# Later low parts, other split points and other slots in a kernel of attention plus product-key experts

## The chip, the cores and the metric

The kernel runs on one core of a Trainium2 chip. Its metric is device time in microseconds (us), the median of several executions. Engines are named as in the profile: PE (TensorE), ACT (ScalarE), DVE (VectorE), POOL (GpSimd), and SP, whose queue issues most of the transfers. Each engine carries out its own instructions strictly in the order in which the program lists them, and waits where an operand or a buffer is not ready.

## What is computed

```python
x = A_x                                   # 2048 tokens x 512
xn = layernorm(x)
A = softmax(q k / 4) v  @ wo              # 32 heads of 16, one key and one value head (k, v = xn @ wk, xn @ wv)

q = einsum("nd,dhc->nhc", xn, w_q)        # 32 heads, 2 x 128
s1, s2 = q[..., :128] @ k1.T, q[..., 128:] @ k2.T      # 64 scores each
# the two best of s1 and the two best of s2 -> 4 sums -> the two best of these: expert i1 * 64 + i2 of 4096
g = softmax(the two sums)
act = gelu(einsum("nd,nhkd->nhk", xn, u[experts]))
B = einsum("nhk,nhk,nhkd->nd", g, act, v[experts])
out = x + A + B
```

## The kernel before

The whole order of instructions is written out by hand. A main loop of 280 steps `d` carries the attention: in a step, `att_steps` computes scores for two key tiles of a unit of four heads and 512 queries, ACT takes their exponentials (`scores`, L448 and L455), and PE adds the previous ones to the output (`pv`, L465). Between these, `fill()` lets one generator, the score thread, go on by about 4 cost units, and `mid()` puts the DVE work of the step in place. What the score thread lists is fixed by its own costs and not by measured times.

The score thread works through `SEQ`: 4 phases of 512 tokens times 8 chunks `c` of 4 heads. For a pair (phase, chunk), `item` computes the 8 x 64 scores of 128 tokens with 12 matmuls (L699): for each quarter k of the 512 features three products of high and low half-precision parts, `TERMS`. DVE then finds the best (MAX8, L712) and their places (FIND_INDEX8, L714) and frees the scores' buffer. `batch` follows each chunk's four items: it turns places into expert numbers with small operations, so far on POOL.

The chunks' weights come from `wp_make`, a generator advanced twice in each item of the chunk before, once after its sixth matmul and once behind it: four steps multiply `w_q` with the keys (L644), four steps (one for each k) transpose the result (L657), and ACT and DVE write its high part (L659) and low part (L660). `wp_square` sums squares of the next chunk's raw weights on ACT (L615). Scores, transposes and most other short products share three PSUM buffers, tag "x" (`xtile`); a new one waits until the oldest content has been read.

Phases 0 and 1 serve the experts by gathering: POOL fetches the rows of one expert choice for 128 tokens, DVE takes a dot product (L1192) and later adds the weighted row (L1227). One such choice is a *slot*, 512 in all; `pos` in the main loop says how many slots may have had their dot by step d, with a rate that depends on `dense_on`, the stage of the score thread.

Phases 2 and 3 serve the experts densely, in `dense`. First `spread` transposes the index and gate tables (L940), then 32 *one-hot* steps `q` build, on DVE, tables of ones (`oh`, `obs`, L973 to L976) that PE multiplies into a gate for every expert (L1012). After that come 32 *blocks* `b` of 128 experts: PE multiplies tokens with a block's u rows (`pact`, L915), ACT and DVE apply gelu and gates, and PE multiplies with the v rows (`pout`, L1058). A block needs its rows split into high and low parts (`half_split`, ACT L874 and DVE L877). In phase 2 the raw rows are fetched (`fetch`, L832 and L833) into one of two buffers; `later_split(b)` splits block b at the next `mid()` and puts `fetch(b + 2)` into the stores of the main step after the next:

```python
        def later_split(b):
            def go():
                split(b)
                store(lambda: store(lambda: fetch(b + 2)))
            on_act(go)
```

If `split(b)` finds that the fetch has not been issued, it issues all waiting stores there and then. In phase 3 the split rows are loaded from memory as phase 2 left them. `SPLITS` names the one-hot steps (NQ = 32) at which the first blocks are split; later ones are split from within the blocks. `dense_on` is 4 and 2 during the last items and the one-hot steps, 3 at their end, 1 in the blocks from b = 4 on, and 0 otherwise. In the program's stores, SP's queue issues transfers in the order in which `run(STORES)` meets them.

Of the kernel before, what the change touches and what calls it, by code (L numbers as in the profile page):

```python
# [23 lines left out]
P = 128  # L24
# [9 lines left out]
NC = 8  # L34
TPH = GT
NPH = NGRP
NSP = 2
# [23 lines left out]
def tile_kernel(ctx, tc, x, wq, wkv, wo, wqT, kT, uv, ub, vb, out):  # L61
    nc = tc.nc
# [4 lines left out]
    late = [None]  # L67
# [6 lines left out]
    raw = lambda ap: ap  # L74
# [4 lines left out]
    d_w = [dram.tile([P, KC, 2, 512], F16, name=f"dw{c}") for c in range(NC)]  # L79
# [55 lines left out]
    XT, XS, XK, XN, ACC, XP = [], {}, {}, {}, {}, [None]  # L135
    STORES, BULK, AFTER, LASTQ = [], [], [], []
    store = STORES.append
# [68 lines left out]
                BULK.append(lambda k=k, xt=xt: nc.sync.dma_start(d_xt[g - 1][k], raw(xt[:])))  # L206

    TERMS = ((0, 0), (0, 1), (1, 0))

    FIRST = ((0, 0), (1, 0), (0, 1))  # L210
    cols = const.tile([P, 40], F32, name="cols")
# [383 lines left out]
    WC = {}  # L595
# [31 lines left out]
    def wk_tile():  # L627
        return big.tile([P, 2, 512], F16, name="wk", tag="wk", bufs=NWK)

    def wp_make(c):  # L630

        wt = [big.tile([P, 2, 512], F32, name="wt", tag="da", bufs=2) for _ in range(2)]
        for h in range(4):
            for n in range(4 * c + h + 1, min(4 * c + h + 5, 4 * NC) if late[0] else 4):
                if ("raw", n // 4, n % 4) not in WC:
                    wp_load(n // 4, n % 4)
            if c == 2 and h > 1:
                wp_square()
            if c > 2 and h == 1:
                wp_factors()  # L640
            w = WC.pop(("raw", c, h))
            p = xtile("pw")
            for s in range(2):
                nc.tensor.matmul(p[s * E:(s + 1) * E, :], kTs[:, s, :], w[:, s, :], start=True, stop=True)  # L644
            nc.scalar.copy(wt[h // 2][:, h % 2, :], p)
            yield 0.9
        WC[c] = []
        if c == 2:
            yield 0.05
            wp_factors()  # L650
            yield 0.05
        for k in range(KC):
            for _ in range((0, 2, 1, 1)[k] if 1 < c < NC - 1 else 0):
                wp_square()
            p = xtile("pwt")
            for h in range(4):
                nc.tensor.transpose(p[:, h * P:(h + 1) * P], wt[h // 2][:, h % 2, k * P:(k + 1) * P], ident)  # L657
            wk = wk_tile()
            nc.scalar.activation(wk[:, 0, :], p, AF.Copy, scale=col(S_W + c))  # L659
            low = lambda p=p, wk=wk: nc.vector.scalar_tensor_tensor(wk[:, 1, :], p, col(S_W + c), wk[:, 0, :],  # L660
                                                                    op0=OP.mult, op1=OP.subtract)
            if c == 1 and late[0] is None:
                AFTER.append(low)
            else:
                low()
            WC[c].append(wk)
            (store if c > 1 else BULK.append)(lambda k=k, wk=wk: nc.sync.dma_start(d_w[c][:, k], raw(wk[:])))
            yield 0.45

    def wp_read(n, ks=range(KC)):  # L670
        for k in ks:
# [9 lines left out]
    def item(n_, ti, make=()):  # L681
        ph, c = SEQ[n_]
        nph, nc_ = SEQ[n_ + 1] if n_ + 1 < len(SEQ) else (None, None)
        t = TPH * ph + ti
        g, j = divmod(t, GT)
        b, jb = divmod(ti, BT)
        if jb == 0:
            m8 = small.tile([P, BT, 8, 8], F32, name="m8", bufs=1)
            i8 = small.tile([P, BT, 8, 8], U32, name="i8", bufs=1)
            M8[ph, c, b], I8[ph, c, b] = m8, i8  # L690
        m8, i8 = M8[ph, c, b], I8[ph, c, b]
        p = xtile("psc")

        more = nc_ is not None and not (ph >= NSP and c == NC - 1)
        read = more and n_ + 1 >= NC
        n = 0
        for k in range(KC):
            for a, bb in TERMS:
                nc.tensor.matmul(p, XT[k][:, a, j * P:(j + 1) * P], WC[n_][k][:, bb, :],  # L699
                                 start=n == 0, stop=n == 11)  # L700
                n += 1
            if read and ti == 0 and k < 2:
                wp_read(n_ + 1, range(2 * k, 2 * k + 2))
            if k < KC - 1:
                yield 3 * UNIT
            if k == 1 or k == 0 and n_ == 1:

                yield from islice(make, 1)
        if more and nph != ph:
            load_xt(nph, j)  # L710
        for s in range(8):
            nc.vector.max(m8[:, jb, s, :], p[:, s * E:(s + 1) * E])  # L712
        for s in range(8):
            nc.vector.max_index(i8[:, jb, s, :], m8[:, jb, s, :], p[:, s * E:(s + 1) * E])  # L714
        if jb == BT - 1:
            batch(ph, c, b)
        yield 3 * UNIT

    IDX, G = {}, {}
# [11 lines left out]
    def batch(ph, c, b):  # L731
# [6 lines left out]
        V = nc.vector  # L738
# [15 lines left out]
            LATER.append(go)  # L754

        fi = T("fi", F32, [P, BT, 8, 2])
        G_ = nc.gpsimd
        G_.tensor_copy(fi, i8[:, :, :, 0:2])  # L758
        fv = fi.rearrange("p t (h s) k -> p t h s k", s=2)
        i1a, i1b, i2a, i2b = fv[:, :, :, 0, 0], fv[:, :, :, 0, 1], fv[:, :, :, 1, 0], fv[:, :, :, 1, 1]  # L760
# [3 lines left out]
        if ph < NSP:  # L764
            idx = T("idx", I32, [P, BT, 4, 2], NIDX)
            i1 = fv[:, :, :, 0, :]
            G_.tensor_scalar(i1, i1, float(E), None, op0=OP.mult)
            G_.tensor_add(e1, i1a, i2b)
            G_.tensor_add(e2, i1b, i2a)
            G_.tensor_add(i1a, i1a, i2a)  # L770
            G_.tensor_sub(e1, e1, e2)
            G_.tensor_mul(e1, e1, cond)
# [51 lines left out]
    def dense(DG, after):  # L824
# [67 lines left out]
# [5 lines that stand above are left out]
# [4 lines left out]
        NQ = 512 // TB  # L901
# [9 lines left out]
        def activations(b, us, p):  # L911
            n = 0
            for k in range(KC):
                for a, c in TERMS:
                    nc.tensor.matmul(p, us[:, a, k * P:(k + 1) * P], XT[k][:, c, :],  # L915
# [53 lines left out]
        def onehot(q):  # L969
            if q < NQ:  # L970
# [6 lines left out]
                OH[q] = oa, ob  # L977

        half = lambda b: on_act(lambda: halves.__setitem__(b, half_split(b, 0)))
        SPLITS = {NQ - 18: lambda: later_split(0), NQ - 15: lambda: later_split(1),  # L980
                  NQ - 12: lambda: half(2), NQ - 10: lambda: later_split(2),
                  NQ - 8: lambda: half(3), NQ - 6: lambda: later_split(3),
                  NQ - 4: lambda: half(4), NQ - 2: lambda: later_split(4)}

        def first_gates():

# [16 lines left out]
        for q in range(NQ):  # L1003
# [5 lines left out]
            p = xtile("pg")  # L1009
            for i in range(TB):  # L1010
                n = 2 if i < TB - 1 else 1
# [24 lines left out]

            if q in SPLITS:
                SPLITS[q]()
            if q == NQ - 3:
# [7 lines left out]
        def sums(group, to):  # L1047
# [5 lines left out]
            for j in range(GT):  # L1053
                p = xtile("pout")
                n, last = 0, 3 * len(group) - 1
                for wd, vs in group:
                    for a, c in TERMS:
                        nc.tensor.matmul(p, wd[0][:, a, j * P:(j + 1) * P], vs[:, c, :], start=n == 0, stop=n == last)  # L1058
# [15 lines left out]
        for b in range(NB):  # L1074
            wd = []
            if b > 1:
                if b not in halved:

                    yield None
                if b not in halved:  # L1080
                    flush()
                p = xtile("pact")
                for k in activations(b, splits[b][0], p):
                    if k == 0:
                        store(lambda b=b: (fetch_gates(b + 1), fetch_gates(b + 2)))
                        if b % 2 == 0 and b > 2:
                            later_split(b + 2)
                        if b == 2:

                            store(load_totals)  # L1090
                    if k == KC - 1 and b == NB - 1 and after is not None:
                        wp_read(after, range(2))
                    if b == NB - 1 and after is not None:
                        load_xt(SEQ[after][0], ks=(k,))
                    if k < KC - 1:
                        yield 3 * UNIT

                if b not in fetched:
                    if formed[0] < b // 2 * 2 - 4:
                        flush()  # L1100
                    run(STORES)
                    assert b in fetched
# [44 lines left out]
            for _ in range(b - 1 if b in (2, 3) else 0):  # L1147
                if out_ready():
                    block_out()
                    yield 3.6  # L1150
            if b % 2 and b > 1:
                later_split(b + 2)
            if b > 4 and b % 4 == 1 or b == NB - 1:
                n = 4 if b < NB - 1 else 2
# [14 lines left out]
    NSL = len(slots)  # L1169
# [92 lines left out]
    def run(fns):  # L1262
        todo = fns[:]
        fns.clear()
        for fn in todo:
            fn()
# [92 lines left out]
    dense_on, quiet = [0], [0]  # L1359
# [215 lines left out]
    with tc.manual_schedule(engines=ENGINES):  # L1575
# [4 lines left out]
        half = STEPS // 2  # L1580
        pos, since = 0.0, half
        for d in range(half + 24):


            if dense_on[0] != 0:
                since = d
            if dense_on[0] == 1:
                pos += 2.5 if d < half * 3 // 4 else max(0.0, NSL - pos) / max(half - 3 - d, 1)
            else:
                pos += (2.5 if len(IDX) < NC * TPH else 2.3 if 0 <= d - since < 32 else 1.75, 0, 0.5, 1.5, 0.5)[dense_on[0]]  # L1590

            todo = max(min(int(pos + 0.001), g_next[0]) - d_next[0], 0) if d else 0

# [74 lines left out]
def build(nc, tc, args):  # L1668
    tile_kernel(tc, *args)
# [33 lines left out]
```

## Time and profile before

| | us |
|---|---|
| median of 3 runs | 1810.38 |
| lowest and highest | 1809.15 and 1815.13 |
| profiled execution, its own time | 1814.29 |
| span in that profile, first to last instruction | 1812.6 |
| PE busy | 1705.5 |
| DVE busy | 1592.4 |
| ACT busy | 1328.8 |
| POOL busy | 685.1 |

The span is cut into 40 slices; digits are tenths of busy time, and PEclk is the granted clock of PE in tenths:

```
PE   7989998999998889999999999999998899999998
DVE  7748898999998976899899899999999868989995
PEclk9999999999999999999999999999998999999999
```

The two darker places of PE in the middle and near three quarters are the one-hot stages. In the answers shown below, a row of the order of time is: start, duration, engine, line, operation, output and input, count, and in brackets the idle time ahead and who ended it. A row of waits is: who waited for whom, total us, times, longest.

### The profile page before, as it was taken

To read this page: it belongs to the slowest core of one execution; us is meant where nothing else is said; L and a number is where in the kernel's file an instruction comes from. 1 tells how busy PE (TensorE), PEld (TensorE's weight loads), DVE (VectorE), ACT (ScalarE), POOL (GpSimd) and SP (SyncE) were. 2 spreads that over 40 slices of the span, in tenths; PEclk is the share of its full clock that TensorE was granted. 3 is DMA by queue.
4 is the path that set the end of the run, shared out by engine and by line. 5 is a ranking of instruction groups with operands and counts; after the bars stand their busy time and mean duration, and the time that the engine had idled before them with its cause. 6 is when DMAs were issued, how large, how long until landed. Compare 5 with 4: busy or idle time off the path is not lost.

```text
span 1812.6 us, 35046 instructions
## 1 busy us (share of the span) xinstructions
PE 1705.5 (94%) x11070; PEld 601.1 (33%) x11070; DVE 1592.4 (88%) x6337; ACT 1328.8 (73%) x1793; POOL 685.1 (38%) x923
## 2 busy tenths in 40 slices
PE   7989998999998889999999999999998899999998
PEld 3433332333333332333333333332333333333332
DVE  7748898999998976899899899999989868989995
ACT  6467787877767886888888666655667877777774
POOL 1034353445543012344344455445541124544440
PEclk9999999999999999999999999999998999999999
DMA  7378788999764567899999976777443789999893
GB/s 260 125 254 308 264 279 282 316 321 324 270 212 139 169 230 260 284 313 341 302 334 345 330 280 237 237 245 245 149 159 131 224 263 293 324 292 332 290 311 114
DMA packets 257273, 470.98 MB, mean 260 GB/s; under 512 B 107316, under 2 KB 118596, under 8 KB 257084
## 3 DMA queue, kind: packets, MB, share of 16 engines
q0 software_dynamic: 73728, 268.47, 43.2%
q1 hardware_dynamic: 182940, 199.59, 34.4%
q8 instruction: 87, 1.43, 0.3%
q14 instruction: 102, 0.84, 0.1%
q10 hardware_dynamic: 416, 0.66, 0.1%
HBM read 407.36 MB, written 56.39 MB: 256 GB/s over the span
## 4 chain that ended last, share of the span: by engine, by line
PE 58%; DVE 20%; ACT 8%; issue 3%; DMA 3%; POOL 1%; SPq 0%; ACTq 0%; DVEq 0%; another core or an unknown queue 0%; POOLq 0%
PE pv L465 17%; PE sc L448 10%; PE psc L699 10%; PE pout L1058 8%; PE pact L915 7%; ACT pt L455 5%; DVE i L714 4%; DVE xa L1227 3%; DVE m L712 3%; DVE g L1192 3%; PE pwo L565 2%; DVE oh L973 2%; PE pw L644 1%; ACT wk L874 1%; DMA rsb<-dinv 1%
## 5 line engine op out<-in xcount | busy, mean ns | idle before, releaser
L455 ACT ACTIVATE pt<-sc 128x1024 f32<-128x1024 f32 x1024 | 990.1, 1026 | 336.6 <-PE sc L448 299.2
L1180 POOL DMA_INDIRECT g<-in_uv_dram,idx x512 | 544.6, 1064 | 896.7 <-DVE xa L1227 367.8
L465 PE MATMUL pv<-pt,vaug 128*32 128x512 f32 x4096 | 503.6, 610 | 0.0
L1227 DVE SCALAR_TENSOR_TENSOR xa<-g,w,xa 128x512 f32<-128x512 f32 x512 | 372.2, 745 | 0.0
L699 PE MATMUL psc<-wk,xt 128*128 128x512 f16 x1536 | 358.4, 381 | 12.5 <-DVE i L714 7.2
L448 PE MATMUL sc<-qa,kaug 64*128 64x512 f16 x2048 | 325.6, 385 | 40.0 <-ACT pt L455 35.3
L1192 DVE CUSTOM_DVE_ANT_0 g<-g,xa 128x512 f32<-128x512 f32 x512 | 334.3, 682 | 2.6 <-DMA g<-in_uv_dram,idx 2.6
L699 PEld LDWEIGHTS <-xt 128*128 128x128 f16 x1536 | 140.9, 98 | 210.9 <-issue 63.0
L448 PEld LDWEIGHTS <-kaug 64*128 64x128 f16 x2048 | 82.0, 94 | 381.7 <-issue 377.9
L714 DVE FIND_INDEX8 i<-m,psc 128x8 uint32<-128x64 f32 x1024 | 206.4, 222 | 0.0
L465 PEld LDWEIGHTS pv<-pt,vaug 128*32 128x32 f32 x4096 | 108.2, 110 | 259.8 <-issue 259.8
L915 PE MATMUL pact<-xt,wk 128*128 128x512 f16 x768 | 184.3, 385 | 4.2 <-DVE wk L877 3.9
L1058 PE MATMUL pout<-wk,wd 128*128 128x512 f16 x768 | 176.5, 380 | 0.0
L712 DVE MAX8 m<-psc 128x8 f32<-128x64 f32 x1024 | 146.1, 214 | 7.9 <-PE psc L699 7.2
L915 PEld LDWEIGHTS <-wk 128*128 128x128 f16 x768 | 69.6, 99 | 105.3 <-issue 29.3
L1058 PEld LDWEIGHTS <-wd 128*128 128x128 f16 x768 | 73.2, 98 | 93.3 <-issue 9.3
L973 DVE TENSOR_TENSOR oh<-io,tr 128x2048 f16<-128x2048 f16 x64 | 77.9, 1218 | 10.0 <-PE pg L1012 4.7
L714 DVE MATCH_VALUE_LOAD i<-m,psc 128x8 f32 x1024 | 72.1, 70 | 0.0
L1131 DVE SCALAR_TENSOR_TENSOR gy<-gy,pact 128x512 f32<-128x512 f32 x60 | 41.0, 683 | 30.2 <-ACT gy L1130 29.0
L1061 DVE SCALAR_TENSOR_TENSOR da<-pout,cols,da 128x512 f32<-128x512 f32 x72 | 53.3, 746 | 15.3 <-PE pout L1058 14.4
L758 POOL CAST fi<-i 128x64 f32<-128x64 uint32 x32 | 8.2, 257 | 141.7 <-DVE i L714 137.9
L1110 DVE SCALAR_TENSOR_TENSOR gy<-gy,gates 128x512 f32<-128x512 f32 x60 | 41.4, 690 | 22.1 <-ACT gy L1132 17.3
(218 smaller groups left out, 1464.6 us busy)
## 6 DMA issues: line engine op xcount, KB each, us to landing
wk<-dw SPq DMA_DIRECT2D x96, 256.0 KB
wqt<-in_wqT_dram SPq DMA_DIRECT2D x32, 512.0 KB
un<-in_uv_dram SPq DMA_DIRECT2D x16, 1024.0 KB
ds<-wk SPq DMA_DIRECT2D x64, 256.0 KB
gates<-dg SPq DMA_DIRECT2D x64, 256.0 KB
wk<-ds SPq DMA_DIRECT2D x64, 256.0 KB
dg<-gst SPq DMA_DIRECT2D x14, 928.0 KB
dw<-wk SPq DMA_DIRECT2D x32, 256.0 KB
```

Of the source, the lines that this page charges most:

```text
L448: nc.tensor.matmul(p[:, b, :], kaug[o:o + 64, kc * P:(kc + 1) * P], QA[u][o:o + 64, i, :], start=True, stop=True)
L455: nc.scalar.activation(PT[u, kc, i], p, AF.Exp, scale=SCALE)
L465: nc.tensor.matmul(PV[u][32 * j:32 * j + 32, :], vaug[:, kc, :], pt[:, b, :], start=kc == 0, stop=kc == 15)
L699: nc.tensor.matmul(p, XT[k][:, a, j * P:(j + 1) * P], WC[n_][k][:, bb, :], start=n == 0, stop=n == 11)
L712: nc.vector.max(m8[:, jb, s, :], p[:, s * E:(s + 1) * E])
L714: nc.vector.max_index(i8[:, jb, s, :], m8[:, jb, s, :], p[:, s * E:(s + 1) * E])
L915: nc.tensor.matmul(p, us[:, a, k * P:(k + 1) * P], XT[k][:, c, :], start=n == 0, stop=n == 11)
L973: nc.vector.tensor_tensor(out=oa, in0=num(P), in1=bc(0, tb, P), op=OP.is_equal)
L1058: nc.tensor.matmul(p, wd[0][:, a, j * P:(j + 1) * P], vs[:, c, :], start=n == 0, stop=n == last)
L1180: nc.gpsimd.indirect_dma_start(out=gt, out_offset=None, in_=uv, in_offset=bass.IndirectOffsetOnAxis(ap=IDX[ph, c, ti][:, s:s + 1], axis=0))
L1192: nc.vector.tensor_tensor_reduce(u, u, XN[TPH * ph + ti], scale=1.0, scalar=0.0, op0=OP.mult, op1=OP.add, accum_out=a[:, i:i + 1])
L1227: nc.vector.scalar_tensor_tensor(acc, v, w[:, i:i + 1], acc, op0=OP.mult, op1=OP.add)
```

## The change

It moves work and changes no product. Low parts and their store are listed one step of `wp_make` later, and a chunk's first item uses the products with new low parts as late as it can (`LOWS_LAST`). Each of the four transposing steps has one `wp_square` instead of none, two, one and one. In the last chunk of phases 2 and 3 the index operations are DVE's instead of POOL's. The splits of the first blocks are put at other one-hot steps: block 4's leaves them for block 2's first step, block 5's comes from block 3's end to its first step. The rates of `pos` change: 2.6 for 2.5 in the blocks, 2.3 for 20 instead of 32 steps after a dense stage, 0.25 for 0.5 in one-hot steps.

```diff
+    LOWS_LAST = ((0, 0, 0), (0, 1, 0), (1, 0, 0), (1, 1, 0), (2, 0, 0), (2, 1, 0),
+                 (0, 0, 1), (1, 0, 1), (3, 0, 0), (3, 1, 0), (2, 0, 1), (3, 0, 1))
...
         for k in range(KC):
-            for _ in range((0, 2, 1, 1)[k] if 1 < c < NC - 1 else 0):
+            run(lows)
+            if 1 < c < NC - 1:
                 wp_square()
...
-            if c == 1 and late[0] is None:
-                AFTER.append(low)
+            if c == 0:
+                low()
             else:
-                low()
+                (AFTER if late[0] is None else lows).append(low)
             WC[c].append(wk)
-            (store if c > 1 else BULK.append)(lambda k=k, wk=wk: nc.sync.dma_start(d_w[c][:, k], raw(wk[:])))
+            keep = lambda k=k, wk=wk: nc.sync.dma_start(d_w[c][:, k], raw(wk[:]))
+            if late[0] is None:
+                BULK.append(keep)
+            else:
+                lows.append(lambda keep=keep: (store if c > 1 else BULK.append)(keep))
             yield 0.45
+        run(lows)
...
-            for a, bb in TERMS:
-                nc.tensor.matmul(p, XT[k][:, a, j * P:(j + 1) * P], WC[n_][k][:, bb, :],
+            for kk, a, bb in LOWS_LAST[n:n + 3] if ti == 0 else [(k, *ab) for ab in TERMS]:
+                nc.tensor.matmul(p, XT[kk][:, a, j * P:(j + 1) * P], WC[n_][kk][:, bb, :],
...
-        G_ = nc.gpsimd
+        G_ = V if ph >= NSP and c == NC - 1 else nc.gpsimd
...
-        SPLITS = {NQ - 18: lambda: later_split(0), NQ - 15: lambda: later_split(1),
-                  NQ - 12: lambda: half(2), NQ - 10: lambda: later_split(2),
-                  NQ - 8: lambda: half(3), NQ - 6: lambda: later_split(3),
-                  NQ - 4: lambda: half(4), NQ - 2: lambda: later_split(4)}
+        SPLITS = {NQ - 16: lambda: later_split(0), NQ - 12: lambda: later_split(1),
+                  NQ - 6: lambda: half(2), NQ - 4: lambda: half(3),
+                  NQ - 2: lambda: later_split(2), NQ - 1: lambda: later_split(3)}
...
-                        if b % 2 == 0 and b > 2:
+                        if b % 2 == 0 or b == 3:
                             later_split(b + 2)
...
-            if b % 2 and b > 1:
+            if b % 2 and b > 3:
                 later_split(b + 2)
...
-                pos += 2.5 if d < half * 3 // 4 else max(0.0, NSL - pos) / max(half - 3 - d, 1)
+                pos += 2.6 if d < half * 3 // 4 else max(0.0, NSL - pos) / max(half - 3 - d, 1)
             else:
-                pos += (2.5 if len(IDX) < NC * TPH else 2.3 if 0 <= d - since < 32 else 1.75, 0, 0.5, 1.5, 0.5)[dense_on[0]]
+                pos += (2.5 if len(IDX) < NC * TPH else 2.3 if 0 <= d - since < 20 else 1.75, 0, 0.25, 1.5, 0.5)[dense_on[0]]
```

More of the change, by code (lines that the diff above doesn't have):

```diff
@@ L646, in wp_make @@
             yield 0.9
-        WC[c] = []
+        WC[c], lows = [], []
         if c == 2:
```

## The prediction

> **What bounds the kernel now.** I read the page's engine table first, then what TensorE waited for, then stretches by stage, then the order of time around each place that the change touches.
>
> ```profile
> span 1812.6 us, 35046 instructions
> PE 1705.5 (94%) x11070; PEld 601.1 (33%) x11070; DVE 1592.4 (88%) x6337; ACT 1328.8 (73%) x1793; POOL 685.1 (38%) x923
> ```
>
> ```profile
> PE sc L448 <- ACT pt L455: 35.3, 65, 2.0
> PE pg L1012 <- DVE obs L976: 16.0, 16, 1.9
> ```
>
> TensorE (PE) is busy 1705.5 of 1812.6 us. The change alters no matmul, only the order of twelve in a chunk's first item, so time comes and goes through PE's 107 idle us and through its clock. The two largest waits are for exps of ScalarE (ACT) and for one-hot tables of VectorE (DVE). Stretches, with the busy us of PE, its weight loads, DVE, ACT and POOL, and then the granted clock:
>
> ```profile
> 194.00:198.00 4.00, 4.00 (x18) 0.96 (x20) 3.86 (x31) 1.84 (x4) 2.25 (x7) 0.57 0.88 283
> 714.00:722.00 8.00, 7.67 (x24) 2.84 (x26) 4.21 (x7) 0.73 (x2) 2.10 (x2) 0.63 0.81 247
> 1252.00:1257.00 5.00, 4.69 (x23) 0.90 (x22) 4.96 (x35) 1.94 (x2) 2.76 (x3) 0.66 0.78 235
> 569.00:667.00 98.00, 80.75 (x958) 32.85 (x957) 90.95 (x164) 83.30 (x105) 7.77 (x7) 0.94 0.52 178
> 1200.00:1346.00 146.00, 139.64 (x850) 46.48 (x852) 143.72 (x935) 86.57 (x106) 76.97 (x149) 0.99 0.61 201
> 1354.00:1450.00 96.00, 82.14 (x965) 33.20 (x967) 84.08 (x153) 80.63 (x98) 10.49 (x8) 0.94 0.54 174
> 1455.00:1790.00 335.00, 333.07 (x2021) 111.58 (x2023) 292.64 (x714) 256.86 (x340) 137.49 (x128) 1.00 0.89 292
> ```
>
> The first three are clock drops behind idle gaps (1.96, 3.88 and 2.01 us long, quoted below): 0.43 of 4 us, 0.37 of 8 and 0.34 of 5, so 1.7, 3.0 and 1.7 us lost beside the gap itself. The one-hot stages (569 to 667, 1354 to 1450) run at 93% and 88% of DVE, the stage from 1200 at 98%, the last dense blocks at 99% of PE.
>
> **Part 1: low parts a step later.** A chunk's weights are made during the four items of the chunk before. Item 2's scores and the transposes of k=0 and k=1 fill the three "x" buffers of PSUM. In the kernel before, k=0's buffer is freed by its low part ahead of item 2's MAX8 and FIND_INDEX8 on DVE. After the change that low part stands behind them in DVE's order, and k=1's later still. So item 3's first matmul, fourth in line for three buffers, has to wait for item 2's last index, and the next chunk's first item for item 3's. The places, as PE and DVE ran them:
>
> ```profile
> 183.65 0.60 PE L657 MATMUL pwt<-ident,wt 128*128 128x128 f32 x4
> 185.17 1.46 PE L699 MATMUL psc<-wk,xt 128*128 128x512 f16 x6 [0.92 <-DVE wk L660]
> 193.83 2.29 PE L699 MATMUL psc<-wk,xt 128*128 128x512 f16 x6 [1.96 <-DVE wk L660]
> 253.65 0.81 PE L699 MATMUL psc<-wk,xt 128*128 128x512 f16 x3 [0.32 <-issue]
> 261.66 0.81 PE L699 MATMUL psc<-wk,xt 128*128 128x512 f16 x3 [1.01 <-DVE wk L660]
> 292.31 0.63 PE L657 MATMUL pwt<-ident,wt 128*128 128x128 f32 x4 [3.38 <-DVE i L714]
> 301.95 1.08 PE L644 MATMUL pw<-wqt,kTs 128*64 128x512 f32 x4 [1.35 <-issue]
> 324.29 0.81 PE L699 MATMUL psc<-wk,xt 128*128 128x512 f16 x3 [0.79 <-DVE wk L660]
> ```
>
> ```profile
> 185.03 1.14 DVE L712 MAX8 m<-psc 128x8 f32<-128x64 f32 x8
> 187.54 0.22 DVE L714 FIND_INDEX8 i<-m,psc 128x8 uint32<-128x64 f32 x1
> ```
>
> An item's eviction lasts from 185.03 to 187.7, 2.65 us; PE has 0.60 us of transposes to put beside it. So each such place becomes a gap of at least 2.05 us, unless an attention block of some 3 us lies between. Against the gaps that stand there now: chunk 3, 2.05 for 0.92 and for 1.96, +1.1 and +0.1; chunk 5, for 0.32 and 1.01, +1.7 and +1.0; chunk 6, where PE stopped for 3.38 us for the same eviction but 1.46 us of matmuls further on, +1.4, and +0.7 over the 1.35; chunk 7, for 0.79, +1.3. Chunks 2 and 4 have attention in between: 0. That is +7.3 with DVE free at once. It began the quoted eviction 1.4 us after the item's end (183.65); with a third of a us at each of seven places it is +9.6. Five of the gaps over 2 us are new (all but the 1.96 and the 3.38), so five clock drops of 1.7: +8.5. While PE is slow DVE catches up, so I take 3 off.
>
> The Trainium skill ("TensorE: Matmul & The Clock Gate", "Why this matters for your kernels") asks for no PE gap over about 3 us, since a window of idling brings the half clock back; by that the five gaps cost no drops and the sum would be 8.5 us less. The 1.96 us gap at 193.83, with 0.57 behind it, speaks against it.
>
> **Part 2: lows last, single squares.** The new order keeps the late low parts of k=2 and 3 from stopping the first item. It gains nothing itself: the quoted waits on L660 stand at first matmuls, which need no new low part; they are waits for the buffer. Two squares in one step hold ACT back:
>
> ```profile
> 228.05 0.39 PE L448 MATMUL sc<-qa,kaug 64*128 64x512 f16 x2 [1.19 <-ACT pt L455]
> ```
>
> One square fewer ahead of this exp takes away most of it, -1; chunk 2 has the like. -2 (0 to -4). Parts 1 and 2: 9.6 + 8.5 - 3 - 2 = **+13** (+3: 7.3 with no drops, less 4 for squares; +18: 9.6 and 8.5 with nothing off).
>
> **Part 3: last index chain on VectorE**, twice.
>
> ```profile
> 561.02 0.31 POOL L758 CAST fi<-i 128x64 f32<-128x64 uint32 x1 [3.30 <-DVE i L714]
> 566.23 0.46 POOL L806 TENSOR_TENSOR da<-hi,ii 128x32 f32<-128x32 f32 x2
> 565.36 0.25 DVE L817 SCALAR_TENSOR_TENSOR da<-gd,gh 128x32 f32<-128x32 f32 x1
> 568.51 1.22 DVE L973 TENSOR_TENSOR oh<-io,tr 128x2048 f16<-128x2048 f16 x1 [2.91 <-issue]
> ```
>
> POOL takes 5.7 us for 15 operations. At L817's 0.25, the dear end of the small DVE operations, 15 are 3.8 us; I take 3. The two index tables come one to two us sooner, but adds, a dot and the gate table (done 565.6) slide by 3 to 568.6, and DVE's first one-hot started at 568.51 before. So PE gets two gaps for one and ends where it was: **0** (-4 to +2 for both). POOL's gathers no longer queue behind the chain; their buffers are freed by DVE, so I count 0 for that.
>
> **Part 4: splits.** Block 5's split goes one block ahead, and its stop at 714 goes. Block 4's goes from the last one-hot steps into block 2's first step, while its raw rows are fetched only two main steps after block 2's split, which now takes the place at ACT's 664.69:
>
> ```profile
> 664.69 0.80 ACT L874 ACTIVATE wk<-rw,cols 128x512 f16<-128x512 f32 x1
> 670.58 1.94 ACT L455 ACTIVATE pt<-sc 128x1024 f32<-128x1024 f32 x2 [0.36 <-PE sc L448]
> ```
>
> ```profile
> 671.38 0.90 SPq L1028 DMA_DIRECT2D dg<-gst  x2
> 675.48 1.00 SPq L861 DMA_DIRECT2D gates<-dg  x2
> 676.53 2.40 SPq L995 DMA_DIRECT2D da<-in_x_dram  x4
> 678.97 0.43 SPq L832 DMA_DIRECT2D rw<-in_ub_dram  x1
> ```
>
> ```profile
> 671.93 3.60 PE L565 MATMUL pwo<-wo,on 128*128 128x512 f32 x8
> 714.33 4.45 PE L915 MATMUL pact<-xt,wk 128*128 128x512 f16 x10 [3.88 <-DVE wk L877]
> ```
>
> SP's queue is in order: what follows the split at 664.69 by two steps is issued behind the gate rows and the totals, at 678.97, as block 6's fetch was. ACT comes to block 4's split one main step after 664.69, ahead of the exps at 670.58. Rows stored from 671.38 to 672.3 could be read at 675.48, so landing takes about 3.2 us: ACT goes on at 682.2, does two splits (0.80 each) and an exp (0.97), and PE, out of work at 675.5 behind L565, gets a score buffer at about 684.9. +9.4, and a clock drop of 1.7. Gone: 3.88 and its 3.0 of clock. **+4** (-7 if ACT does not stop, +8 if landing takes 7 us). The stores that queue behind the fetch are not waited for. In the second dense stage the splits are loads with two blocks to spare: 0.
>
> **Part 5: slots.** A slot is an add and a dot:
>
> ```profile
> L1227 DVE SCALAR_TENSOR_TENSOR xa<-g,w,xa 128x512 f32<-128x512 f32 x512 | 372.2, 745 | 0.0
> L1192 DVE CUSTOM_DVE_ANT_0 g<-g,xa 128x512 f32<-128x512 f32 x512 | 334.3, 682 | 2.6 <-DMA g<-in_uv_dram,idx 2.6
> ```
>
> ```profile
> 1230.68 1.46 PE L699 MATMUL psc<-wk,xt 128*128 128x512 f16 x6 [1.53 <-DVE i L714]
> 1252.31 1.35 PE L699 MATMUL psc<-wk,xt 128*128 128x512 f16 x3 [2.01 <-DVE i L714]
> ```
>
> 0.745 + 0.682 = 1.43 us. One-hot stages: 32 steps, two to a main step, so 16 times 0.25 are 4 slots, 5.7 us of DVE each; block 4's two low parts (0.75 each) leave the first as well. Where DVE is at 93% I take -6, at 88% -3, and -2 for a clock drop saved: -11 (0 to -17, the 16.0 of obs waits and a drop). Steps 20 to 32 after the dense stage: 12 times 0.55 are 6.6 slots, 9.4 us off DVE's 98%; the stops of 1.53 and 2.01 and 1.7 of clock go, and 0.8 of smaller ones: -6 (0 to -8). The slots come back: 0.1 a step over some 44 steps of the first dense blocks (4.4), and 8 + 6.6 - 4.4 = 10 in the last blocks: 14 us on 292.64 of 335, which makes 92%. +2 (0 to +8). **-15** (-25 to +8).
>
> **Sum.** 13 + 0 + 4 - 15 = +2. The profiled execution took 1814.29 us (the span and 1.7 around it), 3.9 above the median of 1810.38; +2 on the median is 1812.4. I say 1813, since the costs are surer than the gains.
>
> **Rivals.** (a) Slower: DVE's relief does not reach PE, because ACT (83.30 of 98 and 80.63 of 96 us in the one-hot stages, and 35.3 us of waits for exps over all) sets the next round. Part 5 then gives -6 instead of -15: 1822. It decides from the point where the 16.0 of obs waits fall by less than half and exp waits take their place. Against it: ACT has 15% left there. (b) Faster: block 4's rows land before ACT asks, part 4 is -7: 1802. For it: an earlier fetch would fit, DMA being half idle in that stage (0.52); against it: SP's order. (c) Faster: gaps of 2 us leave the clock alone, part 1 loses 8.5: 1804. For it: the largest drop stands behind the longest gap; against it: the stretches from 194 and 1252. This is how the clock would go by the rule of the Trainium skill named in part 1.
>
> **Chances.** The forecast (within 0.3%, about 5.4 us, what a measurement of this kernel can tell from no change) 0.38, with a range of its own from 1805 to 1816; (a), or part 1 at its upper end, slower by over 0.3%: 0.34; (b) 0.18 and (c) 0.10, faster: 0.28. The range reaches to 1798, below (b) and (c), and to 1828, (a) with part 1 at +18.
>
> **What would show it.** Right: psc L699 waiting for i L714 by over 10 us more between 125 and 335 us, and its waits for wk L660 gone; ACT stopped some 10 us for a DMA ahead of wk L874 near 670; the 3.88 gone; obs waits near 8 us; the psc stops after 1200 gone. Wrong: no stop of PE between 660 and 700 (b), a clock of 1.00 behind gaps of 2 us (c), one-hot stages as long as before (a).

## The result and the profile after

The changed kernel takes 1821.36 us (median of 9 runs, 1816.76 to 1822.05) where the kernel before took 1811.25 beside it (9 runs, 1808.32 to 1815.13): a ratio of 1.0053, 95% interval 1.0042 to 1.0064. It is slower by some 10 us. One execution of e1, told below, took 3336.08 us, nearly twice as long as all others, and its ratio leaves that one out. The profiled execution of the changed kernel took 1820.91, 6.6 more than that of before.

In the changed file the lines stand a little lower. Old and new numbers: scores L699, now L707; transposes L657, now L660; low parts L660, now L663; weights times keys L644, now L646; FIND_INDEX8 L714, now L722; attention scores L448 and their exps L455, now L450 and L457; splits L874, now L882; one-hot tables L976, now L984; their products L1012, now L1019; a slot's dot L1192 and add L1227, now L1199 and L1234.

The engine table, and then the largest waits of PE with sum, times and longest, both of the changed kernel:

```profile
span 1819.2 us, 35029 instructions
PE 1705.0 (94%) x11070; PEld 599.4 (33%) x11070; DVE 1592.9 (88%) x6367; ACT 1331.1 (73%) x1793; POOL 678.1 (37%) x893
```

```profile
PE sc L450 <- ACT pt L457: 42.8, 65, 11.0
PE psc L707 <- DVE i L722: 18.2, 9, 2.7
...
PE pg L1019 <- DVE obs L984: 8.6, 12, 1.8
PE pwt L660 <- DVE wk L663: 5.7, 4, 2.9
```

Of before, beside the two waits that the prediction shows:

```profile
PE psc L699 <- DVE i L714: 7.2, 6, 2.0
```

Busy time is what it was; PE waits more. Three things have changed places: scores waiting for evictions (`i`) went from 7.2 to 18.2 us, one wait for an exp is now 11.0 us long, and the waits for one-hot tables (`obs`) fell from 16.0 to 8.6.

Where in the span that happened is best read from a mark that both kernels have 32 times: ACT's copy of a finished attention unit. Its start in the profiled executions, as difference to the kernel before (us; the first column is before's own time; the other columns are the changed kernel and four of the experiments told below):

| mark, in before | after | e4, late lows only | e5, slots only | e9, splits only | e14, late lows and slots |
|---|---|---|---|---|---|
| 405.9, weights of chunks 2 to 7 made | +24.7 | +16.0 | -1.8 | +0.7 | +17.6 |
| 608.7, in the first one-hot stage | +22.7 | +16.1 | -3.5 | -0.3 | +16.0 |
| 654.8, near its end | +14.9 | +14.1 | -10.2 | +0.6 | +9.3 |
| 703.4, block 4's split | +30.0 | +14.4 | -10.1 | +16.2 | +9.5 |
| 765.7, block 5's split | +22.7 | +13.4 | -10.7 | +8.9 | +8.2 |
| 1191.4, before the stage from 1200 | +22.0 | +13.3 | -11.1 | +7.1 | +8.5 |
| 1358.1, behind it | +12.9 | +12.9 | -22.4 | +6.6 | -3.0 |
| 1402.8, second one-hot stage | +6.5 | +12.8 | -28.0 | +4.0 | -6.7 |
| 1796.8, end | +6.9 | +12.5 | -26.6 | +3.6 | -6.2 |

Differences of a few us in this table are within the scatter of executions: before's profiled one lies 3.9 above its median.

So the changed kernel loses 25 us while the weights of chunks 2 to 7 are made, regains 8 in the first one-hot stage, loses 15 at block 4's split, regains 7 at block 5's, then 9 in the stage from 1200 and 6 in the second one-hot stage.

The first loss, by PE's waits between 125 and 365 us, before and then after:

```profile
PE psc L699 <- DVE wk L660: 4.7, 4, 2.0
PE sc L448 <- ACT pt L455: 4.2, 6, 1.2
PE pwt L657 <- DVE i L714: 3.4, 1, 3.4
```

```profile
PE psc L707 <- DVE i L722: 16.9, 7, 2.7
PE pwt L660 <- DVE wk L663: 5.5, 3, 2.9
PE pw L646 <- DVE wk L663: 3.7, 1, 3.7
PE psc L707 <- DVE wk L663: 3.1, 1, 3.1
PE sc L450 <- ACT pt L457: 0.5, 1, 0.5
```

The score buffers wait for evictions, as foretold. But there are also 12.3 us (5.5 + 3.7 + 3.1) in which PE waits for the low parts themselves. Two of those waits, in PE's order:

```profile
241.62 1.08 PE L646 MATMUL pw<-wqt,kTs 128*64 128x512 f32 x4 [3.73 <-DVE wk L663]
...
361.51 2.36 PE L707 MATMUL psc<-wk,xt 128*128 128x512 f16 x7 [3.08 <-DVE wk L663]
```

At 241.62 it is the next chunk's product of weights and keys that wants an "x" buffer which a late low part has yet to read. DVE's order shows what that low part stood behind. The item's eviction ended at 235.8; then came index operations, and then the dots and adds of the main step's slots, from 236.62 on:

```profile
236.62 0.68 DVE L1199 CUSTOM_DVE_ANT_0 g<-g,xa 128x512 f32<-128x512 f32 x1
...
240.07 0.74 DVE L1234 SCALAR_TENSOR_TENSOR xa<-g,w,xa 128x512 f32<-128x512 f32 x1
...
240.83 1.40 DVE L663 SCALAR_TENSOR_TENSOR wk<-pwt,cols,wk 128x512 f16<-128x512 f32 x2
```

Ahead of the other four waits for low parts (PE at 156.85, 197.04, 231.13 and 361.51) there are slots too, 2 to 4 us of them. So a late low part stands behind an eviction, behind slots, or behind both. The prediction counted the eviction alone.

From 125 us to the fifth mark (405.9 and 430.6) PE carries out the same 1637 matmuls in both kernels. Its busy time, that of its weight loads, DVE, ACT and POOL, and the granted clock, before and after:

```profile
125.00:405.90 280.90, 265.14 (x1637) 91.40 (x1636) 253.51 (x1380) 220.20 (x319) 124.91 (x174) 0.99 0.88 297
```

```profile
125.40:430.60 305.20, 275.37 (x1637) 92.40 (x1636) 255.24 (x1380) 221.00 (x318) 123.94 (x175) 0.95 0.82 275
```

PE's idle time rose from 15.8 to 29.8 us, by 14.0. Its busy time for the same matmuls rose by 10.2, with the clock at 0.95 where it was 0.99.

The second loss, the fetch of block 4's rows on SP's queue, then ACT, then PE:

```profile
690.68 1.00 SPq L869 DMA_DIRECT2D gates<-dg  x2
691.73 2.22 SPq L1002 DMA_DIRECT2D da<-in_x_dram  x4
693.99 0.43 SPq L840 DMA_DIRECT2D rw<-in_ub_dram  x1
```

```profile
684.96 0.72 ACT L882 ACTIVATE wk<-rw,cols 128x512 f16<-128x512 f32 x1
699.15 1.36 ACT L882 ACTIVATE wk<-rw,cols 128x512 f16<-128x512 f32 x2 [13.47 <-DMA rw<-in_ub_dram]
```

```profile
701.47 0.61 PE L450 MATMUL sc<-qa,kaug 64*128 64x512 f16 x2 [10.99 <-ACT pt L457]
```

At 684.96 ACT takes block 3's last split, then stands 13.47 us before block 4's. Block 4's rows are issued behind gate rows and totals, and land 5.2 us later. PE runs out of exps for 10.99. Block 5's stop (3.88 at 714.33 before) is gone.

### The profile page after: what moved, and what is told of

It is laid out like the page before. It is cut to its first block, busy times and chain, and to the rows that moved or that the text cites. A ratio compares the mean times of both kernels' runs of the same rounds, so it can differ in the third digit from the quotient of the medians.

```text
span 1819.2 us, 35029 instructions
## 1 busy us (share of the span) xinstructions
PE 1705.0 (94%) x11070; PEld 599.4 (33%) x11070; DVE 1592.9 (88%) x6367; ACT 1331.1 (73%) x1793; POOL 678.1 (37%) x893
## 4 chain that ended last, share of the span: by engine, by line
PE 57%; DVE 25%; ACT 6%; issue 3%; DMA 2%; SPq 0%; POOL 0%; ACTq 0%; DVEq 0%; POOLq 0%
PE pv L467 17%; PE psc L707 10%; PE sc L450 10%; PE pout L1065 8%; PE pact L923 7%; DVE i L722 6%; ACT pt L457 4%; DVE m L720 4%; DVE xa L1234 4%; DVE g L1199 3%; DVE oh L981 3%; PE pwo L567 2%; PE pw L646 1%; DVE obs L984 1%; DVE obs L983 1%
## 5 line engine op out<-in xcount | busy, mean ns | idle before, releaser
L457 ACT ACTIVATE pt<-sc 128x1024 f32<-128x1024 f32 x1024 | 990.0, 1025 | 334.2 <-PE sc L450 332.0
L707 PE MATMUL psc<-wk,xt 128*128 128x512 f16 x1536 | 362.6, 385 | 21.4 <-DVE i L722 18.2
L1234 DVE SCALAR_TENSOR_TENSOR xa<-g,w,xa 128x512 f32<-128x512 f32 x512 | 373.3, 745 | 0.1
L450 PE MATMUL sc<-qa,kaug 64*128 64x512 f16 x2048 | 325.8, 386 | 46.0 <-ACT pt L457 42.8
L1199 DVE CUSTOM_DVE_ANT_0 g<-g,xa 128x512 f32<-128x512 f32 x512 | 334.3, 682 | 14.7 <-DMA g<-in_uv_dram,idx 14.7
L707 PEld LDWEIGHTS <-xt 128*128 128x128 f16 x1536 | 141.3, 98 | 222.0 <-issue 55.4
L450 PEld LDWEIGHTS <-kaug 64*128 64x128 f16 x2048 | 82.1, 94 | 386.3 <-issue 381.9
L722 DVE FIND_INDEX8 i<-m,psc 128x8 uint32<-128x64 f32 x1024 | 206.3, 221 | 0.0
L722 DVE MATCH_VALUE_LOAD i<-m,psc 128x8 f32 x1024 | 71.4, 70 | 0.0
L885 DVE SCALAR_TENSOR_TENSOR wk<-rw,cols,wk 128x512 f16<-128x512 f32 x64 | 46.4, 746 | 18.3 <-ACT wk L882 18.3
```

The costliest lines, as they stand in the source:

```text
L450: nc.tensor.matmul(p[:, b, :], kaug[o:o + 64, kc * P:(kc + 1) * P], QA[u][o:o + 64, i, :], start=True, stop=True)
L457: nc.scalar.activation(PT[u, kc, i], p, AF.Exp, scale=SCALE)
L707: nc.tensor.matmul(p, XT[kk][:, a, j * P:(j + 1) * P], WC[n_][kk][:, bb, :], start=n == 0, stop=n == 11)
L1199: nc.vector.tensor_tensor_reduce(u, u, XN[TPH * ph + ti], scale=1.0, scalar=0.0, op0=OP.mult, op1=OP.add, accum_out=a[:, i:i + 1])
L1234: nc.vector.scalar_tensor_tensor(acc, v, w[:, i:i + 1], acc, op0=OP.mult, op1=OP.add)
```

## The experiments

Theories before the runs: the late low parts cost what they cost because they stand behind the eviction in DVE's order; the rival was that the delay, the matmul order or the squares do it. For block 4: the late fetch, against the split's mere place. For the slots: relief of DVE reaches PE, or it doesn't. Unless said otherwise, us against the kernel before are the ratio less 1, times the median of before beside it (1809.78, 1811.56, 1810.52 and 1810.58), and us against the changed kernel are the difference of two such ratios.

**e1: the changed kernel with low parts made at once again** (late order of matmuls and single squares kept)

```
-   if c == 0: low()
-   else: (AFTER if late[0] is None else lows).append(low)
+   if c == 1 and late[0] is None: AFTER.append(low)
+   else: low()
```

> The changed kernel, but a chunk's low parts are listed at once again, in their own step, as in the kernel before; the new order of products in the first item, the later stores, single squares, chain, splits and slots stay. Theory 1 (buffers: a late low part holds one of three x buffers of PSUM until after an item's eviction): the 24 us that the changed kernel is behind at the end of the fifth unit (430.6 against 405.9) go, so about 1797; item matmuls (psc) wait for FIND_INDEX8 by 4 us or less between 125 and 340 us instead of 14.5, and transposes no longer wait for low parts (5.5). Rival 2 (single squares put ScalarE ahead of the transposes' evictions): the time stays near 1821, with the waits where they are.

1798.17, ratio 0.9927 (0.9899 to 0.9954): 23 us below the changed kernel (17 to 28). Its fifth mark is at 407.6, against 430.6 with late low parts and 405.9 before. The waits between 125 and 365 us are of the old size again:

```profile
PE psc L707 <- DVE wk L663: 7.4, 5, 2.0
PE pwt L660 <- DVE i L722: 3.3, 1, 3.3
```

So the lateness of the low parts is the loss of 23 us; the order of the matmuls and the single squares, still in place here, are not.

**e8: the changed kernel, a due low part ahead of the next eviction in DVE's order**

```
+   LOWQ = []            # one list for all chunks
...
-   WC[c], lows = [], []
+   WC[c], lows = [], LOWQ
...
+   run(LOWQ)            # in item(), ahead of MAX8
    for s in range(8): nc.vector.max(...)
```

> The changed kernel, but what low parts are due are listed ahead of an item's MAX8 (or at the next step, whichever comes first), so that each is still later than its own step but a buffer is freed ahead of the eviction. Theory 1 (buffers): waits of item matmuls for FIND_INDEX8 fall from 14.5 to under 6 us, the time to about 1802. Rival 3 (low parts are missed as operands, by the first item's products): late as before, so no change, 1819 to 1823.

1793.13, ratio 0.9925 (0.9895 to 0.9955): 23 us below the changed kernel (17 to 29), more than the 19 that were expected. Waits between 125 and 365 us:

```profile
PE psc L708 <- DVE wk L664: 9.9, 8, 2.6
PE pwt L661 <- DVE wk L664: 1.9, 2, 1.2
```

The low parts are still queued and not made at once; but a due one now stands ahead of the eviction, and so also ahead of the slots that are listed behind that eviction. This is enough to take the loss away, so it is their place in DVE's order that costs. How much of it is the eviction and how much the slots, e8 doesn't part: by the waits in the changed kernel, 16.9 us end with an eviction's last index and 12.3 with a low part. Between e1 and e8 the intervals overlap.

**e2: the changed kernel, block 4's rows fetched one main step sooner**

```
-   store(lambda: store(lambda: fetch(b + 2)))
+   store((lambda: fetch(b + 2)) if b == 2 else lambda: store(lambda: fetch(b + 2)))
```

> The changed kernel, but the raw rows of block 4 are fetched one main step sooner: after block 2's split the fetch goes into the next step's stores, not into those after. Nothing else differs. Theory 1 (order of SP's queue: the fetch stands behind gate rows and totals): the stop of 10.99 us at 701.5 goes or falls under 2, with its clock drop: 1821 - 12 = 1809. Rival (the raw buffer is not free, or DMA is full, so the fetch lands late wherever it stands): the stop stays over 6 us, 1817 or more.

1811.79, ratio 1.0013 (0.9999 to 1.0027): 7 us below the changed kernel (4 to 10), where 12 were expected. The fetch now stands at

```profile
676.48 0.35 SPq L840 DMA_DIRECT2D rw<-in_ub_dram  x1
```

and block 4's splits go through without a stop; a shorter one comes at block 5's, whose rows are issued at 691.69, on ACT and PE:

```profile
699.57 1.55 ACT L882 ACTIVATE wk<-rw,cols 128x512 f16<-128x512 f32 x2 [4.15 <-DMA rw<-in_ub_dram]
```

```profile
702.69 0.61 PE L450 MATMUL sc<-qa,kaug 64*128 64x512 f16 x2 [4.74 <-ACT pt L457]
```

So the stop is the fetch's place in SP's queue, and 11.0 becomes 4.7. By the marks it is worth 6.9: e2 is 4.8 ahead of the changed kernel at the mark of 654.8 and 11.7 at that of 703.4. The 4.8 are none of its doing. Up to there e2 is the changed kernel itself, yet its fifth mark is at 425.5, 5.1 earlier, by the clock (last section).

**e4: before with late low parts and their matmul order alone**

```
+   run(lows)            # at the head of each transpose step k, and after the last
...
-   if c == 1 and late[0] is None: AFTER.append(low)
-   else: low()
+   if c == 0: low()
+   else: (AFTER if late[0] is None else lows).append(low)
...
-   for a, bb in TERMS:
+   for kk, a, bb in LOWS_LAST[n:n + 3] if ti == 0 else [(k, *ab) for ab in TERMS]:
```

> The kernel before with the late low parts and the first item's order alone. Theory 1 (buffers): about +24 us, 1835, nearly all of it between 125 and 370 us, with new stops over 2 us and a clock drop behind each. Rival 2 (the loss needs single squares with it): +13 or less, 1824 or less.

1828.15, ratio 1.0120 (1.0077 to 1.0162): +22 us (14 to 29), about the 24 that were expected; in the profiled execution 16.0 of it stands at the fifth mark. Waits of PE between 125 and 365 us:

```profile
PE psc L707 <- DVE i L722: 16.9, 7, 2.7
PE pwt L660 <- DVE wk L663: 4.5, 3, 1.9
PE pw L646 <- DVE wk L663: 3.6, 1, 3.6
PE psc L707 <- DVE wk L663: 3.1, 1, 3.1
```

These are the same places as in the changed kernel, and but for one nearly the same sizes. Over the same 1637 matmuls PE idles 29.7 us here and 29.8 there, so the idle part of the first loss is all this edit. What differs is the other part: PE's busy time for them is 268.0 us here, with a clock of 0.98, and 275.4 there, with 0.95.

**e5: before with the new slot rates alone**

```
-   pos += 2.5 if d < half * 3 // 4 ...        +   pos += 2.6 ...
-   2.3 if 0 <= d - since < 32 else 1.75, 0, 0.5, 1.5, 0.5
+   2.3 if 0 <= d - since < 20 else 1.75, 0, 0.25, 1.5, 0.5
```

> The kernel before with the new rates of slots alone (2.6, 20 steps, 0.25). Theory 1 (VectorE is what the one-hot stages and the stage from 1200 us wait for, so slots taken from there become PE's time): about -14, 1796; waits for obs tables from 16.0 to about 8 us, no stops of item matmuls after 1200. Rival (a) (exps pace the one-hot rounds): -6 or less, 1804 or more, with exp waits of PE up by what the obs waits lose.

1789.05, ratio 0.9883 (0.9859 to 0.9907): -21 us (17 to 26), more than the 14 that were expected. The stage from 1200 and the second one-hot stage, to be held against before's rows in the prediction:

```profile
1200.00:1346.00 146.00, 142.12 (x945) 49.48 (x943) 141.37 (x850) 98.30 (x122) 73.79 (x141) 1.00 0.53 171
1354.00:1450.00 96.00, 87.20 (x874) 33.38 (x876) 75.96 (x143) 81.12 (x98) 10.21 (x8) 0.98 0.65 209
```

DVE had 143.72 of 146 us there before, and 84.08 of 96; PE had 139.64 and 82.14. By the marks the stage from 1200 gives 11.3, the first one-hot stage 6.7, the second 5.6; from there to the end, where the slots are put back, 1.5 go again. Between the marks on both sides of the stage from 1200, with the same 969 matmuls, before and then e5:

```profile
1191.40:1358.10 166.70, 157.53 (x969) 53.56 (x967) 159.36 (x1002) 100.99 (x125) 86.70 (x165) 0.98 0.59 191
```

```profile
1180.30:1335.70 155.40, 153.65 (x969) 52.76 (x967) 150.59 (x961) 101.12 (x124) 80.60 (x159) 1.00 0.58 188
```

DVE's work falls by 8.8 us and the time by 11.3: PE's idle time by 7.4, and its busy time for the same matmuls by 3.9, as the clock goes from 0.98 to 1.00.

**e6: before with the last index chain on DVE alone**

```
-   G_ = nc.gpsimd
+   G_ = V if ph >= NSP and c == NC - 1 else nc.gpsimd
```

> The kernel before with the last index chain on VectorE alone. Theory 1 (two shorter gaps for one, the first one-hot starts when it did): 0, from -3 to +1; the stops of 3.40 and 2.57 us before the table transposes become pieces of 1.2 and one of 2.1, and their clock drops go at most once. Rival (the chain on GpSimd is what the stage starts after): -5 or more, as both stops go whole.

1810.19, ratio 1.0002 (0.9985 to 1.0019): nothing, within 3 us. PE's one gap of 3.40 in the transposes of the tables, here in the kernel before,

```profile
566.75 1.54 PE L940 MATMUL ptd<-ident,da 128*128 128x128 f32 x6 [3.40 <-POOL da L806]
```

is three of 1.2 in the changed kernel, two of which are

```profile
587.81 0.63 PE L948 MATMUL ptd<-ident,da 128*128 128x128 f32 x4 [1.22 <-DVE da L814]
589.64 0.65 PE L948 MATMUL ptd<-ident,da 128*128 128x128 f32 x4 [1.21 <-DVE gy L936]
```

**e7: before with single squares alone**

```
-   for _ in range((0, 2, 1, 1)[k] if 1 < c < NC - 1 else 0):
+   for _ in range(1 if 1 < c < NC - 1 else 0):
```

> The kernel before with one square a step alone. Theory 1: the waits for exps at 152.8 and 228.1 lose one square each, -2, from 0 to -4, within what can be told from none. Rival 2 (a square ahead of the first transposes' eviction holds the buffers): slower by over 3.

1809.46, ratio 0.9996 (0.9981 to 1.0011): too little to tell from nothing.

**e9: before with the new split points alone**

```
-   NQ - 18: later_split(0), ..., NQ - 6: later_split(3), NQ - 4: half(4), NQ - 2: later_split(4)
+   NQ - 16: later_split(0), NQ - 12: later_split(1), ..., NQ - 2: later_split(2), NQ - 1: later_split(3)
...
-   if b % 2 == 0 and b > 2: ... later_split(b + 2)
+   if b % 2 == 0 or b == 3: ... later_split(b + 2)
...
-   if b % 2 and b > 1: later_split(b + 2)
+   if b % 2 and b > 3: later_split(b + 2)
```

> The kernel before with the new split points alone. Theory 1 (the changed kernel's trace: block 4's fetch stops PE for 11 us, block 5's stop of 3.9 goes, with what their clock drops are worth): +8, 1820, from 1816 to 1823. Sum of the five parts run alone would then be +18 - 1 + 0 - 22 + 8 = +3, against the +10 of all together. Rival (the stop is caused by the parts together, as the one-hot steps run faster there and leave the fetch less time): 0 or less.

1813.87, ratio 1.0016 (1.0002 to 1.0029): +3 us (0.4 to 5), under the +8 (1816 to 1823) that was expected and above the rival's 0. The stop is there in full, without any other edit:

```profile
687.83 0.61 PE L448 MATMUL sc<-qa,kaug 64*128 64x512 f16 x2 [11.74 <-ACT pt L455]
```

By the marks the splits cost 15.6 at block 4, give back 7.3 at block 5, and stand at +8.9 there, much as in the changed kernel (15.0 and 7.2); over the rest of the span 5.3 of that goes again, in small steps, some of which may be the scatter between executions (the profiled one was the slowest of 11, 1808.74 to 1817.85).

**e14: before with late low parts and the new slots, nothing else.** The parts by themselves sum to +22 - 21 + 0 - 1 + 3 = +3, all together gave +10; does anything cost more in company? (The figures named in the expectation are from medians and marks, not ratios.)

```
e4's edit and e5's edit
```

> Before plus the late low parts (with lows last) plus the new slot rates, nothing else; the two alone gave +18 and -22 us, all five edits together +10, so some 14 us are in no single part. If late low parts and slots add, 1811 + 18 - 22 = 1807 (1803 to 1811), and the 14 us belong to the splits within the changed kernel (a stop of ScalarE of 11 us where alone it cost 3). If the two work against each other (the slots moved out of the one-hot stages lie beside the weights' chains and make the late low parts dearer), it comes to 1815 to 1821, the unit ends of chunks 3 to 6 lag by more than the 16 of the low parts alone, and the splits cost no more than their 3. Between 1811 and 1815: both have a share.

1808.44, ratio 0.9992 (0.9977 to 1.0008): -1 us (-4 to +1), against a sum of +1 by ratios. Low parts and slots add. What parts e14 from the changed kernel is the splits, the squares and the chain, some 11 us; by the marks 9 come at blocks 4 and 5 (the changed kernel is 5.6 behind e14 at the mark of 654.8 and 14.5 at that of 765.7), and 7 stand there before 560, where the two differ in single squares alone. e2, with single squares too, is only 2.0 behind e14 at that place, so most of the 7 is scatter of the clock. e2 also bears on the 11 us: with block 4's fetch made sooner and all else left in place, 7 of them go. What the other 4 are, and why the splits cost only 3 alone, isn't settled.

**e10, e11, e13: versions that take what paid.** e10 is e8 with the old split points for blocks 0 to 4 and block 5's split kept early; e11 is the kernel before with the new slots and block 5's split at block 3's first step; e13 is e11 with e8's order of low parts.

```
e10, on e8:  SPLITS as before;  if b % 2 == 0 and b > 2 or b == 3: ... later_split(b + 2)
e11, on before:  e5's rates;    if b % 2 == 0 and b > 2 or b == 3: ... later_split(b + 2)
                                if b % 2 and b > 3: later_split(b + 2)
e13, on e11:  low parts queued, run ahead of MAX8 and of the next transpose step
```

> The changed kernel with due low parts ahead of an item's MAX8 (as in the run before), and with the splits of the kernel before in the one-hot steps (block 4 among them); block 5's stays one block sooner. Theory 1 (block 4's fetch stopped ScalarE for 11 us, block 5's late split stopped PE for 3.9): both stops go, 12 us under the run with low parts ahead (1793): 1781, from 1778 to 1786; PE has no stop over 3 us between 600 and 720. Rival (the fetches only stand behind one another, and the stop moves to block 5 or 6 as it did with the fetch one step sooner): 1788 or more.

> The kernel before with the new rates of slots, and with block 5's split one block sooner and nothing else. Theory 1: the stop of 3.89 at 704 and its clock drop go from the run of slots alone (1789): 1782, from 1780 to 1785. Rival (ACT or the fetch then stops elsewhere): 1788 or more.

> The run with slots and block 5, and with due low parts ahead of an item's MAX8 and at the latest one step later. Theory 1 (VectorE no longer stands before a low part that ScalarE has not readied, while a buffer is still freed ahead of the eviction): -4 against the run without it, 1778, with fewer stops between 125 and 335 us. Rival (what is won on VectorE is lost to buffers held longer): within 2 of the run without it.

e10: 1783.24, ratio 0.9849 (0.9829 to 0.9870). e11: 1780.70, ratio 0.9837 (0.9823 to 0.9850). e13: 1780.12, ratio 0.9841 (0.9827 to 0.9855). None has a stop of PE over 3 us between 600 and 720. e10 and e11 came as expected. The 4 us that were expected of e13 did not come: it doesn't differ from e11, so once low parts are not held behind an eviction and slots, it is all one whether they are made at once or a step later. Both beat the kernel before by some 29 us and the changed one by some 39. e11's engine table:

```profile
span 1779.0 us, 35039 instructions
PE 1689.7 (95%) x11070; PEld 598.4 (34%) x11070; DVE 1588.0 (89%) x6337; ACT 1329.2 (75%) x1793; POOL 690.2 (39%) x923
```

## Why the prediction came out as it did

The forecast was 1813, within 0.3%; the time is 1821.36, in the case that held 0.34. The kernel got slower, as forecast, but by 10 us and not 2. The forecast's mechanisms are in the trace; one term of its sum was too small.

- **Part 1, the term that failed.** It stood in the sum with 15 (9.6 + 8.5 - 3), and with 13 beside the squares. Measured, it is +22 by itself (14 to 29) and +23 within the changed kernel (17 to 28, by e1). What was counted came as counted: seven gaps of 2.0 to 2.7 us in which scores wait for `i`, 16.9 us where 4.7 + 3.4 stood before, 8.8 net for 9.6. What was not counted are 12.3 us of waits for the late low parts themselves, since on DVE these stand behind slots as well as behind the eviction. Of the 12.3, 8.1 fall on chunks 2 and 4 (2.92, 1.44 and 3.73), for which the prediction put 0 because attention lies between. Part 2's sentence, that lows last keeps the late low parts from stopping the first item, holds but for one first item (the 3.08 at 361.51). The 3 us taken off because DVE would catch up show in no row. Less what exps and other waits gave back, PE's idle time grew by 14.0, where 9.6 - 3 - 2 makes 4.6. The clock's 8.5 lies within what the profiles show for the stage: 10.2 in the changed kernel's, 5.9, 4.0 and 2.8 in those of e2, e14 and e4. The sign to look for came: `psc` waits for `i` by over 10 us more, and of its waits for `wk` one is left, for another reason.
- **Squares and chain** (parts 2 and 3), -2 and 0: neither can be told from nothing when alone (e7, e6).
- **Part 4, splits.** The mechanism held to the row: the fetch behind gate rows and totals, ACT stopped, 3.88 gone. The gap was 10.99 for 9.4, since landing took 5.2 us and not 3.2. Net +8 by the marks for +4; +3 by itself. Rival (b), rows that land in time, is what e2 had to make by hand.
- **Part 5, slots**, -21 by itself for -15. One-hot stages gave 12 (6.7 + 5.6 in e5) for 11; the stage from 1200 gave 11.3 for 6, 7.4 of it idle time of PE and 3.9 busy time as the clock rose, where the prediction had 4.3 of stops and 1.7 of clock; of the +2 for slots put back 1.5 came.
- **Rival (a)**, relief of DVE that doesn't reach PE, fell: the `obs` waits fell by 7.4 of 16.0, a little less than half, but without the stop of 10.99 the exp waits are 31.8 where they were 35.3, so nothing took their place, and by the marks the one-hot stages are 8 and 6 us shorter.
- **Rival (c)**, gaps of 2 us that leave the clock alone, holds in some gaps and executions and not in others (below).

In sum, by the changed kernel's marks: 22.7 to the one-hot stage, -7.7 in it, +15.0 and -7.2 at the splits, -0.7, -9.1 in the stage from 1200, -6.4 in the second one-hot stage, +0.4, which is +6.9 for +2. That the time is no further from the forecast is in part luck: part 1 cost some 7 us more than its 15, and part 5, which gave 6 more than its 15, hid most of that.

## What to carry to other kernels

A buffer that several producers share is freed in the order of the engine that reads it. Before a read is made later, list all that stands between the old place and the new one on that engine (here an eviction of 2.65 us and 2 to 4 us of slots), and count the waits of every user of the buffer, not only of the one that was looked at. A split that is moved nearer to the one that frees its raw buffer has to take its fetch along, past all that stands in the queue ahead. Work taken from an engine that was at 98% in a stage paid in full here: 8.8 us of DVE's work for 11.3 of time. And an edit of five parts may hide a gain of 29 us in a loss: time the parts alone.

## What the runs showed of the hardware

Whether a gap of 2 us takes the clock down is not a matter of the gap alone. Shown are the four us behind gaps of 2.40, 1.99 and 2.40 us of PE in the changed kernel, and behind the same three gaps in e2 (2.40, 2.00 and 2.40), which is the same program up to there (the clock is the third number from the end):

```profile
189.60:193.60 4.00, 4.00 (x28) 1.22 (x30) 1.24 (x4) 2.37 (x4) 0.00 (x0) 1.00 0.75 245
...
199.70:203.70 4.00, 4.00 (x14) 1.05 (x18) 3.86 (x15) 0.63 (x1) 2.46 (x9) 0.50 0.99 377
276.40:280.40 4.00, 4.00 (x19) 0.88 (x23) 3.22 (x12) 2.03 (x3) 2.51 (x9) 0.58 0.39 135
```

```profile
188.80:192.80 4.00, 3.99 (x28) 1.23 (x30) 1.24 (x4) 2.37 (x4) 0.00 (x0) 1.00 0.71 248
198.90:202.90 4.00, 4.00 (x28) 1.22 (x30) 3.86 (x15) 1.94 (x2) 2.38 (x9) 1.00 0.99 343
...
272.90:276.90 4.00, 4.00 (x29) 1.13 (x30) 3.48 (x15) 2.40 (x4) 2.51 (x9) 1.00 0.39 135
```

Behind the second of these gaps the clock was halved in one execution and whole in the other, and behind the third it was 0.58 and 1.00; e2 was 5.1 us ahead at the fifth mark. So in these rows a drop behind such a gap is a chance and not a price. The prediction's five times 1.7 us lies within what the profiles show for the whole stage: the busy time of PE for the same 1637 matmuls was 10.2, 5.9, 4.0 and 2.8 us above that of before in the changed kernel, e2, e14 and e4. The Trainium skill ("TensorE: Matmul & The Clock Gate", "What's actually happening") says that the gate looks at a window that runs free of the program, and that runs differ for that reason; these rows fit that, though they don't show the window. The same page's rule in "Why this matters for your kernels", no gap over some 3 us, does not hold here as a safe bound: the clock was 0.50 behind 1.99 us.
